# Eight experts on one core: four VectorE sums moved from the third to the fourth pair of column tiles, and a rare path moved from the middle to the end

## The chip, the cores and the metric

The kernel runs on one core of a Trainium2 chip, in one launch. The core has five engines that run their own instruction streams and meet at semaphores: TensorE (PE; its weight loads are shown as PEld), VectorE (DVE), ScalarE (ACT), GpSimd (POOL) and SyncE (SP, which here only issues DMA). The metric is the device time of one execution in microseconds (us). Before the change it is 427.3 us, the median of three runs (424.16, 427.3 and 427.44).

## The reference

Two stages follow each other. A gated recurrence, for 4 batches of 8 heads, gives 3072 tokens of 384 numbers; then every token is sent to one of 8 experts and through that expert's two layers:

```python
for t in range(S):                       # S = 768, head size 48
    state = alpha[:, :, t, :, None] * state + einsum('bhd,bhe->bhde', k[:, :, t], v[:, :, t])
    y[:, :, t] = einsum('bhd,bhde->bhe', q[:, :, t], state)
x = y as (3072, 384)
logits = normalized(x) @ normalized(expert_emb).T / tau      # 8 experts
expert_idx = argmax(logits); gate_w = softmax(logits)[expert_idx]
for e in range(8):
    mask = expert_idx == e
    h = maximum(x[mask] @ w1[e], 0.0)    # 384 -> 1024
    out[mask] = gate_w[mask, None] * (h @ w2[e])             # 1024 -> 384
```

All of it is float32.

## The kernel before, in words

**Stages.** Up to about 186 us the kernel computes the recurrence in 24 chunks of 128 tokens, chooses the experts, and writes each token's row to a place of its expert in a DRAM tensor `xs`. From there on `run(i)` works through the experts, i = 0 to 7, in an order of turns. The change lies in this second part; what follows is about it.

**One expert.** An expert has 384 rows (three tiles of 128), fetched from `xs` ahead of time. If it has more, `run_extra(i)` after it computes one further half block of 64 rows, behind a branch that every engine takes by a value read from memory (`values_load` of `extra`, L1156, and `tc.If`, L1160). With these data three of the eight experts take that half block: the first, the fourth and the fifth (i = 0, 3 and 4). The body that the other five jump over is 128 matmuls and 128 weight loads on TensorE. If an expert had more than one such half block, `run_rest` (L1164 to L1205) would compute the rest in a loop, behind one branch on `most` (L1169, L1173). With these data its body is never run. In the kernel before it stands after the fourth expert (i = 3); in program order there are four experts behind it.

**First layer, in pairs.** For i = 1 to 7, `first_layer_pair` (called at L1121) computes two of the eight 128-column tiles of the hidden layer, f and f + 4, with one of Strassen's schemes in place of the plain product: eleven products of 128x192, each two matmul records long in the trace, into four PSUM banks a, b, c, d. There are four such pairs, f = 0 to 3. The banks are drained by VectorE adds (`add`, at L919 in the trace, since the helper `by_dve` records them) and ScalarE copies and rectifiers (L1004, L1007). Each bank has a single buffer, so a later product into bank d waits for the add that reads d:

```python
product(c, s3, t3, True, False)
add(u3, c, u2)
filled(1)
product(d, c2, xT[:, 2, r2], True, False)
product(d, s1, t1, False, False)
add(h2[:, r2], d, u3)
filled(1)
...
product(d, s4, xT[:, 1, r2], False, False)
```

**The sums of the columns.** The second layer of two of the three tiles of rows is Strassen's scheme as well (`second_layer_pair`), and needs sums and differences of the hidden layer's columns, `hT_m`: four VectorE operations with two operands in SBUF for two values of f at a time (`mix_hidden`, 128x256 each). They wait in a list `fill`, and `filled(n)`, called inside `first_layer_pair`, takes n of them from the list: one, one and two in a pair. What is left at the end of the fourth pair is done there. `by_dve` ties every VectorE operation of this part to the one before it, so that they run in the order in which they are written.

**Beside it.** GpSimd computes sums of the second layer's weights for the same expert, `w2_m` (`mix_weights`, L943): eight operations on 128x384, from SBUF to SBUF, tied behind the last scatter of the expert before (`done_pair`). Between the pairs, TensorE turns a tile of the next expert's rows and VectorE copies it (`prepare`). After the fourth pair come the third tile of rows in plain form (`second_layer`, L903), the pair of tiles (L1044), and, on VectorE, the sums for the next expert's first layer (`mix_first`, L973).

Of the kernel before, what the change touches and what calls it, by code (L numbers as in the profile page):

```python
# [27 lines left out]
def kernel(  # L28
# [14 lines left out]
    E, DM = expert_emb.shape  # L43
# [8 lines left out]
    FT = F // P  # L52
# [76 lines left out]
    NW = 3  # L129
# [24 lines left out]
    def blocks_run(i):  # L154

        return NC - EARLY if i == 0 else NC

    def slots(i):
        return [(t, P) for t in range(blocks_run(i))] + [(blocks_run(i), HALF)]
# [40 lines left out]
    with ExitStack() as c1:  # L200
# [482 lines left out]
        for s in range(NS + 3):  # L683
# [57 lines left out]
            if 4 <= s < 4 + NXG * (NC + 1):  # L741
                i, t = divmod(s - 4, NC + 1)
# [39 lines left out]
    with ExitStack() as c3:  # L782
# [45 lines left out]
        def turn_of(calls):  # L828
            queue = ExitStack()
            for call in calls:  # L830
                queue.enter_context(tc.issue_after(call.ins))
            return queue
# [43 lines left out]
        def prepare(i, t, by=None):  # L876
            _, n = slots(i)[t]
            return turn(xg_s[i % NXG][:, t], xT_s[i % 2][:, :, t * P : t * P + n], n, by)

        def prepare_gates(i):  # L880
            n = len(slots(i))
            return gates(
                xg_s[i % NXG][:, 0:n], gt_s[i % NG][:, 0:n], sx_s[i % NG][:, 0:n], n,
                used[:, i, 0:n],
            )

        def first_layer(w1_t, hT, xT, f, n):

            ph = bank()[:, 0:n]
            for i in range(KT):  # L890
                nc.tensor.matmul(
                    ph, lhsT=w1_t[:, i, f * P : (f + 1) * P], rhs=xT[:, i],
                    start=(i == 0), stop=(i == KT - 1),
                )
            return nc.scalar.activation(hT[:, f], ph, AF.Relu)
# [19 lines left out]
        fill = []  # L915

        def by_dve(call, *args):
            with turn_of(dve):
                dve[:] = [call(*args)]  # L919
            return dve[0]  # L920

        def filled(n):
            for _ in range(min(n, len(fill))):
                fill.pop(0)()
# [8 lines left out]
        def mix_weights(w2_t, j):  # L933

            (b11, b12), (b21, b22) = quarters(w2_t)
            t1, t2, t3, t4 = (w2_m[:, k] for k in range(4))
            to, x, y = ((t1, b12, b11), (t2, b22, t1), (t4, b21, t2), (t3, b22, b12))[j]

            n = FT // 4
            with turn_of(done_pair):  # L940
                for k in range(2):
                    f = slice(k * n, k * n + n)
                    nc.gpsimd.tensor_tensor(to[:, f], x[:, f], y[:, f], ALU.subtract)  # L943

        def mix_hidden(hT, f0, f1):

            a11, a12, a21, a22 = (
                hT[:, j * FT // 2 + f0 : j * FT // 2 + f1, i * P : i * P + P]
                for i in range(2) for j in range(2)
            )  # L950
            s1, s2, s3, s4 = (hT_m[:, k, f0:f1] for k in range(4))
            for to, x, y, op in (
                (s1, a21, a22, ALU.add), (s2, s1, a11, ALU.subtract),
                (s4, a12, s2, ALU.subtract), (s3, a11, a21, ALU.subtract),
            ):
                yield lambda to=to, x=x, y=y, op=op: by_dve(nc.vector.tensor_tensor, to, x, y, op)
# [151 lines left out]
        def run(i):  # L1108

            w1_t, w2_t = w1_s[i % NW], w2_s[i % NW]  # L1110
            xT = xT_s[i % 2]
            n = blocks_run(i) * P
            nxt = slots(i + 1) if i + 1 < E else []
            hT = hp.tile([P, FT, NC * P], FP32, name="hT")[:, :, 0:n]
            pair = blocks_run(i) == NC
            dve[:] = [] if pair else ready
            if pair:
                for j in range(4):
                    mix_weights(w2_t, j)
                for f in range(FT // 2):  # L1120
                    done = first_layer_pair(w1_t, hT, xT, f)  # L1121
                    if f < len(nxt):
                        turned = prepare(i + 1, f, by_dve)
                    if f % 2 == 1:
                        fill.extend(mix_hidden(hT, f - 1, f + 1))
                filled(len(fill))
            else:
                for f in range(FT):
                    done = first_layer(w1_t, hT, xT[:, :, 0:n], f, n)
                    if f % 2 == 1 and f // 2 < len(nxt):  # L1130
                        turned = prepare(i + 1, f // 2)
            if nxt:
                with turn_of(dve):
                    mix_first(i + 1)
            if nxt:
                with tc.issue_after(done.ins), tc.issue_after(turned.ins):
                    prepare_gates(i + 1)
            else:

                with turn_of(done_pair):  # L1140
                    drained.append(nc.gpsimd.drain())
            gate, col = gt_s[i % NG], sx_s[i % NG]
            for t in range(2 if pair else 0, blocks_run(i)):
                sent = second_layer(
                    w2_t, hT[:, :, t * P : (t + 1) * P], gate[:, t : t + 1], col[:, t : t + 1]
                )
            if not pair:

                done_pair.append(sent)
            if pair:  # L1150
                second_layer_pair(w2_t, hT, gate, col)
# [14 lines left out]
        def run_rest(free):  # L1166

            w1_t, w2_t = w1_s[free], w2_s[free]
            big = nc.values_load(  # L1169
                most, min_val=0, max_val=N // HALF,  # L1170
                skip_runtime_bounds_check_because="the half blocks of an expert",
            )
            with tc.If(big > 1):  # L1173
                nc.sync.dma_start(out=turns[0:1], in_=extra)
                nc.sync.dma_start(out=turns[1:2], in_=turn_i)
                with tc.For_i(0, E) as i:

                    cur = yp.tile([1, 2], I32, name="cur", bufs=1)
                    for j in range(2):
                        nc.sync.dma_start(  # L1180
                            out=cur[0:1, j : j + 1], in_=turns[j : j + 1, ds(i, 1)]
                        )
                    e = nc.values_load(
                        cur[0:1, 1:2], engines=(SP,), min_val=0, max_val=E - 1,
                        skip_runtime_bounds_check_because="a sum of two experts, less E from E on",
                    )
                    nc.sync.dma_start(
                        out=w1_t, in_=w1_r[ds(e, 1)].rearrange("e p k f -> (e p) k f")
                    )
                    nc.sync.dma_start(  # L1190
                        out=w2_t, in_=w2_r[ds(e, 1)].rearrange("e p k d -> (e p) k d")
                    )
                    n = nc.values_load(
                        cur[0:1, 0:1], min_val=0, max_val=N // HALF - 2 * NC,
                        skip_runtime_bounds_check_because="the half blocks of an expert",
                    )
                    with tc.For_i(1, n) as u:
                        xg = yp.tile([P, 1, ROW], FP32, name="xg1", bufs=1)
                        nc.vector.memset(xg, 0.0)
                        nc.sync.dma_start(  # L1200
                            out=xg[0:HALF, 0], in_=xs[ds(e * N + u * HALF + NC * P, HALF)]
                        )
                        xT = yp.tile([P, KT, HALF], FP32, name="xT1", bufs=1)
                        turn(xg[:, 0], xT, HALF)
                        gate = yp.tile([P, 1], FP32, name="gate1", bufs=1)  # L1205
                        col = yp.tile([P, 1], I32, name="col1", bufs=1)
                        gates(xg, gate, col, 1)
                        half_block(w1_t, w2_t, xT, gate[0:HALF], col[0:HALF])
# [14 lines left out]
        for i in range(E):  # L1223
            if i + 2 < E:
                weights(i + 2)
                to_rows(pads[:, i + 2 : i + 3], blank)
                fetch(i + 2)
            run(i)
            run_extra(i)
            if i == 3:  # L1230
                run_rest(i % NW)


# [28 lines left out]
```

## Time and profile before

| what | measured |
|---|---|
| time, median of 3 | 427.3 us |
| span of the profiled execution | 428.2 us |
| TensorE matmul / weight load / VectorE / ScalarE / GpSimd busy | 97 / 85 / 64 / 42 / 45 % of the span |
| first expert product to the end | from about 180 to 428.2 us |

The times from the first product of a pair to the first product of the next one, in us (the last column to the first product of `second_layer`), read from the timeline of TensorE:

| expert | f = 0 | f = 1 | f = 2 | f = 3 | half block in f = 0 |
|---|---|---|---|---|---|
| i = 1 | 9.77 | 3.91 | 4.63 | 4.14 | yes (that of i = 0) |
| i = 2 | 4.29 | 3.90 | 3.91 | 4.00 | no |
| i = 3 | 4.29 | 3.91 | 4.24 | 4.00 | no |
| i = 4 | 10.89 | 3.90 | 5.55 | 4.01 | yes (that of i = 3) |
| i = 5 | 9.81 | 3.90 | 4.63 | 4.00 | yes (that of i = 4) |
| i = 6 | 4.29 | 3.91 | 3.90 | 4.00 | no |
| i = 7 | 7.89 | 3.58 | 3.57 | 3.58 | no |

The last expert has no rows of a next one to turn, so its pairs are some 0.33 us shorter. An expert's branch on `extra` lies behind the first products of the next expert, which is why the half block shows up in the next expert's f = 0.

How to read such a profile here: TensorE is busy nearly all of the time, so a change of the time has to show as a change of the gaps between its matmuls, or of the end behind the last of them. Work on the other engines counts only where a TensorE instruction waits for it.

### The profile page before, as it was taken

Reading aid. Unit: us, or ns where it says so; the run is one execution under the profiler, and the core shown is the slowest. Engines: PE = TensorE matmul, PEld = TensorE weight load, DVE = VectorE, ACT = ScalarE, POOL = GpSimd, SP = SyncE. Lnnn points to the kernel's source line nnn. Section 1 sums busy time; section 2 is a strip of 40 time slices with the busy share of each in tenths; the row PEclk is TensorE's granted clock in tenths of the full one; section 3 lists DMA queues with packets and bytes.
Section 4 is the critical chain, followed back from the end, with each engine's and each line's share of the span. In section 5 each row is a group of like instructions: output and inputs, shape, how many; then the busy total and the mean of one; then the engine's idle time right before and its main releaser. Section 6 shows DMA issues by size and latency. Waiting matters only on the chain. (4 is left out here: it accounts for less than half of the span.)

```text
span 428.2 us, 10643 instructions
## 1 busy us (share of the span) xinstructions
PE 414.1 (97%) x3962; PEld 365.2 (85%) x3962; DVE 274.4 (64%) x725; ACT 178.1 (42%) x430; POOL 191.6 (45%) x283
## 2 busy tenths in 40 slices
PE   8999999999999999999999999999899999997995
PEld 6988888898899876889799799798789979977984
DVE  7898788788798323816846837824862784782531
ACT  4455554554455335443523523613341362360410
POOL 7355776677765537208027036016302702604401
PEclk9999999999999999999999999999999999998999
DMA  9999999999979814869009129017304601001001
GB/s 141 157 159 160 149 209 162 213 182 211 194 167 342 315 63 132 269 222 337 2 35 344 38 60 349 8 50 273 96 20 155 237 2 55 2 14 40 0 17 38
DMA packets 119371, 60.15 MB, mean 140 GB/s; under 512 B 102287, under 2 KB 113816, under 8 KB 119312
## 3 DMA queue, kind: packets, MB, share of 16 engines
q1 hardware_dynamic: 115208, 49.14, 49.4%
q0 software_dynamic: 3728, 10.16, 6.7%
q8 instruction: 38, 0.62, 0.7%
q14 instruction: 21, 0.17, 0.1%
q10 hardware_dynamic: 376, 0.05, 0.1%
HBM read 49.69 MB, written 11.45 MB: 143 GB/s over the span
## 5 line engine op out<-in xcount | busy, mean ns | idle before, releaser
L814 POOL DMA_INDIRECT out_dram<-y,sx x25 | 24.4, 977 | 162.1 <-DVE xT_m L973 73.4
L996 PE MATMUL pq<-xT,w 128*128 128x192 f32 x280 | 65.6, 333 | 3.2 <-PEq L1160 2.6
L996 PEld LDWEIGHTS pq<-xT,w 128*128 128x128 f32 x280 | 48.2, 193 | 5.4 <-issue 3.5
L919 DVE TENSOR_TENSOR hT<-pq,v 128x192 f32<-128x192 f32 x84 | 29.8, 355 | 32.5 <-PE pq L996 30.1
L507 POOL TENSOR_TENSOR qs<-qc,a 128x512 f32<-128x512 f32 x24 | 30.6, 1276 | 35.9 <-DVE a L503 22.0
L903 PE MATMUL pyo<-w,hT 128*128 128x384 f32 x128 | 43.3, 492 | 0.0
L996 PE MATMUL pq<-xT_m,w_m 128*128 128x192 f32 x168 | 36.9, 329 | 0.3 <-PEq L1173 0.3
L903 PEld LDWEIGHTS pyo<-w,hT 128*128 128x128 f32 x128 | 23.7, 190 | 15.3
L1004 ACT ACTIVATE hT<-hT 128x384 f32<-128x384 f32 (+1 forms) x56 | 24.8, 443 | 26.9 <-DVE hT L919 22.3
L479 DVE TENSOR_TENSOR_SCAN r<-pa,inr 128x511 f32<-128x511 f32 x24 | 29.2, 1217 | 7.6 <-PE pa L194 5.9
L503 DVE TENSOR_TENSOR_SCAN a<-pa,ini 128x512 f32<-128x512 f32 x24 | 29.3, 1223 | 1.1
L996 PEld LDWEIGHTS pq<-xT_m,w_m 128*128 128x128 f32 x168 | 29.1, 192 | 0.6 <-issue 0.6
L1044 PE MATMUL pq<-w_m,hT_m 128*128 128x192 f32 x168 | 29.6, 326 | 0.0
L943 POOL TENSOR_TENSOR w_m<-w 128x384 f32<-128x384 f32 x28 | 27.7, 1011 | 3.6 <-DMA xs<-blank,pads 1.9
L1004 ACT ACTIVATE hT<-pq 128x192 f32<-128x192 f32 x28 | 9.2, 330 | 47.7 <-PE pq L996 47.7
L191 PE MATMUL sc<-qs,kr 64*128 64x128 f32 x384 | 28.7, 290 | 0.0
L313 POOL DMA_INDIRECT xs<-x,dest x24 | 24.4, 1016 | 8.2 <-issue 4.3
L1044 PEld LDWEIGHTS pq<-w_m,hT_m 128*128 128x128 f32 x168 | 27.7, 190 | 0.0
L191 PEld LDWEIGHTS sc<-qs,kr 64*128 64x128 f32 x384 | 24.1, 193 | 4.2 <-issue 3.0
L943 POOL TENSOR_TENSOR w_m<-w,w_m 128x384 f32<-128x384 f32 x28 | 27.1, 996 | 0.0
L191 PE MATMUL pyx<-sm,vt 128*64 128x128 f32 x384 | 26.3, 279 | 0.0
L1051 DVE SCALAR_TENSOR_TENSOR y<-pq,gt,u 128x192 f32<-128x192 f32 x21 | 8.8, 418 | 26.5 <-PE pq L1044 26.5
(199 smaller groups left out, 906.9 us busy)
## 6 DMA issues: line engine op xcount, KB each, us to landing
w<-in_moe_w_dram SPq DMA_DIRECT2D x16, 1536.0 KB
kt<-in_k_dram SPq DMA_DIRECT2D x24, 192.0 KB
qt<-in_q_dram SPq DMA_DIRECT2D x24, 192.0 KB
vt<-in_v_dram SPq DMA_DIRECT2D x24, 192.0 KB
xg<-xs SPq DMA_DIRECT2D x22, 196.5 KB
at<-in_alpha_dram SPq DMA_DIRECT2D x24, 168.0 KB
xg<-xs SPq DMA_DIRECT2D x8, 98.2 KB
at<-in_alpha_dram SPq DMA_DIRECT2D x24, 22.5 KB
```

The costliest lines, as they stand in the source:

```text
L191: last["pe"] = nc.tensor.matmul(*args, **kwargs)
L313: ins = nc.gpsimd.indirect_dma_start(out=xs, out_offset=bass.IndirectOffsetOnAxis(ap=rows, axis=0), in_=x, in_offset=None, bounds_check=E ...
L479: nc.vector.tensor_tensor_scan(r[:, L - 2 :: -1], pa[:, L - 1 : 0 : -1], inr[:, L - 2 :: -1], 1.0, ALU.mult, ALU.add,)
L503: d["a_scan"] = by_dve = nc.vector.tensor_tensor_scan(a, pa, ini, 0.0, ALU.mult, ALU.add)
L507: by_pool = nc.gpsimd.tensor_tensor(qs.rearrange("p n t -> p (n t)"), d["qc"], a, ALU.mult)
L814: ins = nc.gpsimd.indirect_dma_start(out=out, out_offset=bass.IndirectOffsetOnAxis(ap=col, axis=0), in_=y, in_offset=None, bounds_check=N - 1,
L903: pe[:] = [nc.tensor.matmul(py, lhsT=hT[:, f], rhs=w2_t[:, f], start=(f == 0), stop=(f == FT - 1),)]
L919: dve[:] = [call(*args)]
L943: nc.gpsimd.tensor_tensor(to[:, f], x[:, f], y[:, f], ALU.subtract)
L996: pe[:] = [nc.tensor.matmul(to, lhsT=left, rhs=right, start=start, stop=stop, skip_group_check=True,)]
L1004: return nc.scalar.activation(h, p, AF.Relu)
L1044: pe[:] = [nc.tensor.matmul(to, lhsT=left[:, f], rhs=right[:, f], start=start and f == 0, stop=stop and f == n - 1, skip_group_check=True,)]
```

## The change

The first edit moves the first group of four column sums: before, they were put into the list after f = 1, and so done during f = 2. Now they are put there after f = 2 and done during f = 3. The second group, of f = 2 and 3, is done after the fourth pair in both versions. The second edit moves `run_rest` behind the last expert, with that expert's weight buffer as the free one.

```diff
                     done = first_layer_pair(w1_t, hT, xT, f)
                     if f < len(nxt):
                         turned = prepare(i + 1, f, by_dve)
-                    if f % 2 == 1:
-                        fill.extend(mix_hidden(hT, f - 1, f + 1))
+
+                    if f >= FT // 4:
+                        f0 = 2 * (f - FT // 4)
+                        fill.extend(mix_hidden(hT, f0, f0 + 2))
                 filled(len(fill))
...
             run(i)
             run_extra(i)
-            if i == 3:
-                run_rest(i % NW)
+        run_rest((E - 1) % NW)
```

FT is 8, so `f >= FT // 4` holds for f = 2 (which puts in the sums of f = 0 and 1) and f = 3 (those of f = 2 and 3). The first edit is for another spread of VectorE's work over the pairs, the second for taking a path that is hardly ever used out of the middle of the program.

## The prediction

> **What bounds the kernel now.** I read the page's busy times first, then TensorE's waits from 180 us on (the experts), then what stands around each wait.
>
> ```profile
> PE 414.1 (97%) x3962; PEld 365.2 (85%) x3962; DVE 274.4 (64%) x725; ACT 178.1 (42%) x430; POOL 191.6 (45%) x283
> PE pq L996 <- PEq L1160: 2.6, 1, 2.6
> PE pq L996 <- DVE hT L919: 2.3, 3, 1.4
> PE pq L996 <- PEq L1173: 0.3, 1, 0.3
> ```
>
> TensorE is the bound. In the expert part it has three kinds of gap, and each concerns this change: a wait for VectorE's adds inside the pairs, one wait of 2.6 us at the branch on `extra` (L1160), one of 0.3 us at the branch of `run_rest` (L1173). Nothing else on TensorE can be won here.
>
> The gap inside the pairs is explained by what VectorE does just ahead of it. Expert i = 4, third pair (VectorE, then GpSimd, then TensorE):
>
> ```profile
> 300.41 2.49 DVE L919 TENSOR_TENSOR hT_m<-hT 128x256 f32<-128x256 f32 x1
> 302.82 0.34 DVE L919 TENSOR_TENSOR hT<-pq,v 128x192 f32<-128x192 f32 x1
> 300.67 1.94 POOL L943 TENSOR_TENSOR w_m<-w 128x384 f32<-128x384 f32 x2
> 303.22 0.92 PE L996 MATMUL pq<-xT,w_m 128*128 128x192 f32 x4 [1.38 <-DVE hT L919]
> ```
>
> The first moved sum takes 2.49 us; it ends when GpSimd's last `w2_m` operation ends (302.61). The add behind it, which frees bank d, comes late, and TensorE stands for 1.38 us. Over all experts the sums' median is 415 to 420 ns, but the first two of a group take up to 2487 and 950 ns, all in third pairs:
>
> ```profile
> L919 DVE TENSOR_TENSOR hT_m<-hT x28: 415/419/2487, 201.2 to 410.7; 128x256 f32<-128x256 f32 x28
> L919 DVE TENSOR_TENSOR hT_m<-hT_m,hT x14: 407/416/950, 203.0 to 409.9; 128x256 f32<-128x256 f32 x14
> ```
>
> The 2.6 us gap is one slow branch among eleven on TensorE's queue (minimum, median, maximum in ns), at 389.6 us; the next timeline row shows TensorE's restart, with matmuls at half their pace:
>
> ```profile
> L1160 PEldq COMPARE_BRANCH  x11: 70/193/3817, 182.6 to 421.2; - x11
> 393.61 0.98 PE L996 MATMUL pq<-xT,w 128*128 128x192 f32 x2 [2.63 <-PEq L1160]
> q8 instruction: 38, 0.62, 0.7%
> ```
>
> The other jumped branches on this line took 338 to 412 ns. The DMA line says why one could take ten times as long: 38 packets of 16 KB of instructions were fetched while the kernel ran, and one of them starts 1.0 us after this branch and ends 1.6 us before TensorE goes on.
>
> [...]adds with one operand in PSUM kept 0.36 us beside the same GpSimd work. [...]The eight matmuls from 393.6 to 396.3 us follow each other at 0.32 us and more, twice their usual 0.16.
>
> **Part 1, the sums.** Nothing is added or removed on any engine; four sums per expert (i = 1 to 7) go from f = 2 to f = 3. By the last `w2_m` operation's end, GpSimd is done before f = 3 starts in every expert: 202.49 against 204.18, 233.88 against 234.79, 263.91 against 265.59, 302.61 against 304.30, 339.32 against 341.01, 370.59 against 371.47, 400.90 against 404.88. So in f = 3 the sums take 0.42 us each. What they delay: in f = 3 VectorE has five adds of 0.36, one copy of 0.36 and now four sums of 0.42, together 3.84 us of the pair's 4.00. That is tight, but two of the sums stand behind the last add. And the trace has a case without contention: in i = 7, f = 2 has these sums at 0.41 us and is 3.57 us long, as its f = 3 without them (3.58). So TensorE loses nothing in f = 3. Behind f = 3 VectorE is about 0.83 us later (two sums). The first wait for it is the second product of the pair of tiles, 6.6 us after the end of f = 3 (for i = 5 from 345.01 to 351.57), while the last `hT_m` is done at 347.3, then at 348.2. `mix_first` ends at 352.0, then 352.8; the next adds start at 353.14 now, after 0.84 us of idle. The scatter behind L906 moves by as much; GpSimd has nothing else then. Cost: nothing. Gain: f = 2 falls to the 3.90 us of an undisturbed pair: 0.73 (i = 1) + 0.01 + 0.34 (i = 3) + 1.65 (i = 4) + 0.73 (i = 5) + 0 + 0 = 3.46 us.
>
> **Part 2a, the middle.** Expert i = 4's first pair takes 10.89 us; those of i = 1 and 5, with the same half block and no `run_rest`, 9.77 and 9.81. Taking the loads and branches out gives 1.1 us. The listing of the instructions also shows the last two `xs<-blank,pads` scatters move from behind that branch to the six at 163 to 170 us, where GpSimd then idles 2.49 us: 2 x 1.29 = 2.58, so the early tokens' scatter may start some 0.4 us later, and nobody waits for it. In f = 0 of i = 4, `w2_m` starts about 1 us earlier.
>
> **Part 2b, the slow branch.** [...]I counted instructions in the two compiled TensorE programs. The branch of `extra` jumps 259 instructions[...]. In the program before, the jumped branches of i = 1, 2, 5, 6, 7 stand at 5534, 6148, 8324, 8938 and 9512: modulo 256 at 158, 4, 132, 234 and 40. Only 234 was slow[...]. In the program after they stand at 159, 6, 59, 162 and 225.[...] The second reading, that a block had just begun and its successor wasn't there yet, or that labels don't count, puts i = 7 (225, or exactly the old place if labels fall away) in danger, but not i = 1, 2, 5 or 6; i = 7's branch has no matmul behind it. So the stall leaves the path. It is worth more than its gap: 7.89 us against the 3.96 that f = 0 of i = 6 (4.29) would have without its turn of 0.33; that is 3.93 us, the rest being the half clock.
>
> **Part 2c, the end.** After the change each engine reads `most` (269 to 311 ns in the middle) and jumps before the final waits. TensorE's jump there is 329 instructions from place 232: it likely [...]takes 3.8 us, from about 423.4 to 427.2 on the old time scale. Today the end is set by the last scatter's landing at 426.7 and ten SP waits to 427.3; TensorE would come through just then. GpSimd gains a load, a branch and a semaphore step (0.2 to 1.0 us) beside the same landing. I take +0.4 us; the bounds are 0 and +2 (both TensorE branches slow, or GpSimd's step in full with its 2.0 us drain behind).
>
> **Sum.** -3.46 - 1.1 - 3.93 + 0.4 = -8.1 us: 427.3 becomes 419.2.
>
> **Rivals.** (A) The slow fetch doesn't go but falls on another mid-program branch[...]: -3.46 - 1.1 + 0.4, 423.1 us.[...] Against it: four known places. (B) The third pair's gain is given back in the fourth, where VectorE's margin is 0.16 us: -1.1 - 3.93 + 0.4, 422.7. Against it stands i = 7. (C) The sums are not hidden in f = 3 at all: 7 x 4 x 0.42 = 11.8 us, and the end costs 2: -8.5 + 11.8 + 2 = +5.3, 432.6, slower. For it: 3.84 of 4.00 us; against it: the same load in f = 2 with a larger copy (i = 2) caused no gap, even with stretched sums.
>
> **How the numbers follow.** Forecast 0.75, (A) 0.10, (B) 0.07, (C) 0.05, unknown 0.03. The bounds of the end and of part 1 (a run of before came in at 424.2) give 416.8 to 421.5 for the forecast; with (A) and (B) the range is 416.8 to 423.4. Faster by over 1% means below 423.0: 0.82; same 0.12; slower 0.06.
>
> **What would show it.** All `hT_m` sums at 0.41 to 0.43 us; f = 2 at 3.9 us in each expert; f = 3 unchanged at 4.0; i = 4's f = 0 near 9.8; i = 7's near 4.0 with no branch over 0.5 us before 420 us; a slow branch on the `most` line at the end. It would be wrong with new TensorE waits for L919 in f = 3, a 3.8 us branch in mid-program, or a tail over 7 us behind the last matmul (5.3 now).

## The result and the profile after

The kernel after takes 420.02 us (median of four runs, 419.12 to 420.91) against 426.85 us for the kernel before on the same chip (four runs, 424.16 to 427.44). The ratio is 0.9852, with a 95% interval of 0.9804 to 0.9900: 6.8 us faster, where the forecast was 8.1.

The spans of the two profiled executions differ by more, 428.2 against 418.6 us: the trace of before is of an execution of 430.28 us, longer than all four timed ones, that of after of one of 420.33. They split as follows; each number is a difference of start or end times of TensorE's products in the two traces.

| stretch | before | after | difference |
|---|---|---|---|
| start to the first product of the pairs (i = 1) | 185.87 | 184.01 | -1.86 |
| from there to the end of the last product | 237.01 | 228.00 | -9.01 |
| from there to the end | 5.28 | 6.62 | +1.34 |

The change doesn't touch the first stretch; it varies between executions and chips, so what follows compares the second, called the **expert part**, and the third, the **tail**. The expert part by pairs (lengths from the first product of one pair to that of what follows, in us):

| pair | i = 1 | 2 | 3 | 4 | 5 | 6 | 7 |
|---|---|---|---|---|---|---|---|
| f = 0 before | 9.77 | 4.29 | 4.29 | 10.89 | 9.81 | 4.29 | 7.89 |
| f = 0 after | 9.65 | 4.28 | 4.29 | 9.66 | 9.66 | 4.29 | 3.96 |
| f = 2 before | 4.63 | 3.91 | 4.24 | 5.55 | 4.63 | 3.90 | 3.57 |
| f = 2 after | 3.91 | 3.91 | 3.90 | 3.91 | 3.90 | 3.91 | 3.57 |

f = 3 is 4.00 us in i = 1 to 6 of the kernel after and 3.58 in i = 7, as before (i = 1 had 4.14 then).

A part of this table isn't the change's. The half block in the first pairs of i = 1, 4 and 5 takes TensorE 5.74 to 5.91 us in the trace of before, but 5.62 each time in the kernel after and in every trace below but three; those three, from a second chip, have 5.70 to 5.96.

The busy times of the page of the kernel after and its line on instruction packets:

```profile
PE 408.0 (97%) x3962; PEld 361.1 (86%) x3962; DVE 267.9 (64%) x725; ACT 178.6 (43%) x430; POOL 191.3 (46%) x283
q8 instruction: 38, 0.62, 0.6%
```

The counts are what they were. VectorE's busy time has fallen by 6.5 us, though it does the same operations; TensorE's has fallen by 6.1, of which some 2.5 lie ahead of the pairs. The answer for the tile `hT_m` of the kernel after (minimum, median, maximum in ns) says where VectorE's fall comes from; these two groups have lost 6.45 us:

```profile
L919 DVE TENSOR_TENSOR hT_m<-hT x28: 411/416/419, 203.1 to 400.0; 128x256 f32<-128x256 f32 x28
L919 DVE TENSOR_TENSOR hT_m<-hT_m,hT x14: 411/414/424, 203.7 to 399.2; 128x256 f32<-128x256 f32 x14
```

The maxima of 2487 and 950 ns are gone: no sum in any expert is stretched. VectorE's timeline of i = 4, fourth pair, in the kernel after:

```profile
299.90 0.41 DVE L919 TENSOR_TENSOR hT_m<-hT 128x256 f32<-128x256 f32 x1
300.23 0.35 DVE L919 TENSOR_TENSOR hT<-pq,v 128x192 f32<-128x192 f32 x1
300.50 0.41 DVE L919 TENSOR_TENSOR hT_m<-hT_m,hT 128x256 f32<-128x256 f32 x1
```

The sum takes 0.41 us and the add that frees a bank follows at once. TensorE's waits from 180 us on have no row left in this trace: none for L919, none for a branch. TensorE's timeline at the start of i = 7 shows the place of the old 2.6 us gap:

```profile
383.23 0.81 PE L996 MATMUL pq<-xT_m,w_m 128*128 128x192 f32 x4
384.19 0.56 PE L996 MATMUL pq<-xT,w 128*128 128x192 f32 x2
```

0.15 us lie between the end of the first row and the start of the second, where 2.63 us were, and the products go on at their usual pace. The branches on TensorE's queue in the kernel after (L1162 is `extra`, L1175 is `most`, now at the end):

```profile
L1162 PEldq COMPARE_BRANCH  x11: 70/297/698, 180.8 to 410.3; - x11
L1175 PEldq COMPARE_BRANCH  x1: 1480/1480/1480, 412.6 to 412.6; - x1
```

The 3817 ns branch is gone from the middle. At the end there is one of 698 ns and one of 1480, not one of 3.8 us.

### The profile page after: what moved, and what is told of

Same layout as the page of the kernel before. It is cut to its first block, busy times and chain, and to the rows that moved or that the text cites. A ratio compares the mean times of both kernels' runs of the same rounds, so it can differ in the third digit from the quotient of the medians.

```text
span 418.6 us, 10657 instructions
## 1 busy us (share of the span) xinstructions
PE 408.0 (97%) x3962; PEld 361.1 (86%) x3962; DVE 267.9 (64%) x725; ACT 178.6 (43%) x430; POOL 191.3 (46%) x283
## 5 line engine op out<-in xcount | busy, mean ns | idle before, releaser
L996 PE MATMUL pq<-xT,w 128*128 128x192 f32 x280 | 64.5, 328 | 0.6
L919 DVE TENSOR_TENSOR hT<-pq,v 128x192 f32<-128x192 f32 x84 | 30.0, 357 | 32.8 <-PE pq L996 30.8
L996 PEld LDWEIGHTS pq<-xT,w 128*128 128x128 f32 x280 | 47.3, 190 | 2.8 <-DVEq L1162 1.7
L919 DVE TENSOR_TENSOR v<-pq,v 128x192 f32<-128x192 f32 x56 | 19.9, 356 | 9.1 <-ACT v L1007 4.4
```

What stands on the lines that cost most here:

```text
L996: pe[:] = [nc.tensor.matmul(to, lhsT=left, rhs=right, start=start, stop=stop, skip_group_check=True,)]
```

## The experiments

Each kernel is compared with the kernel before in runs on the same chip; the runs with two, four and sixteen idle products come from a second chip, the other experiments from a first. Five kernels do exactly the work of before or after, with only a few idle products put ahead of everything: they shift TensorE's code. "Place" is an instruction's number in the compiled TensorE program modulo 256, a count chosen by the author; in the traces of before and after 261 and 260 of TensorE's instructions start per 16 KB instruction packet (4171 from 16.17 to 145.12 us and 4159 from 16.30 to 143.96 us, over sixteen packets each, ahead of the first jump). From the sixteen idle products on it is counted without labels (the marks in the program to which branches jump), for a reason that appears there.

### Each half of the change by itself

The sums' edit alone, with the rare path left behind the fourth expert:

```diff
-                    if f % 2 == 1:
-                        fill.extend(mix_hidden(hT, f - 1, f + 1))
+                    if f >= FT // 4:
+                        f0 = 2 * (f - FT // 4)
+                        fill.extend(mix_hidden(hT, f0, f0 + 2))
```

> The sums are moved to the fourth pair, and run_rest stays behind i = 3. My theory: all hT_m sums take 0.41 to 0.43 us, f = 2 is 3.9 us in every expert, f = 3 stays at 4.0; that is 3.5 us. The first pair of i = 4 stays near 10.9. Each expert has one TensorE instruction more than before, so the branch of i = 6 stands at 240 of a block and not at 234. [...]f = 0 of i = 7 is 4.0 and the time is about 419.5 us. Rival (a block was entered just before, and its successor had not been fetched): the branch at 240 is still slow, over 2.5 us, and the time is about 423.4.

Measured: 419.9 us (before 426.88; ratio 0.9844, 0.9812 to 0.9877). Expert part 228.94 us, tail 5.26, f = 2 at 3.90 us in i = 1 to 6; the first pair of i = 4 takes 10.61 us, not 10.9. This kernel's answers on the tile `hT_m` and on the line of `extra`:

```profile
L919 DVE TENSOR_TENSOR hT_m<-hT x28: 412/415/419, 202.7 to 400.5; 128x256 f32<-128x256 f32 x28
```

The sums are as short as in the whole change.

```profile
L1162 PEldq COMPARE_BRANCH  x11: 70/197/415, 180.3 to 410.8; - x11
```

And the slow branch is gone too: the longest of the eleven, that of i = 6, now at place 240 instead of 234, took 415 ns.

The rare path's move alone:

```diff
-            if i == 3:
-                run_rest(i % NW)
+        run_rest((E - 1) % NW)
```

> run_rest at the end, the sums in the third pair as before. My theory: sums of up to 2.5 us in f = 2, f = 2 longer than 3.9 in some experts as before (3.4 us in all, less in i = 4, where w2_m starts earlier), no slow branch before the end (the jumped branches stand at 158, 4, 54, 156, 218), f = 0 of i = 4 at 9.7, and an end about 1.3 us longer than that of the kernel before: about 423 us. Rival (the gain of the change is all in the sums): about 427.

Measured: 423.53 us (ratio 0.9934, 0.9898 to 0.9969), expert part 231.06, tail 6.64. This kernel's answer on the tile `hT_m`:

```profile
L919 DVE TENSOR_TENSOR hT_m<-hT x28: 410/419/1577, 198.8 to 402.5; 128x256 f32<-128x256 f32 x28
```

Its branches on the lines of `extra` and `most`:

```profile
L1160 PEldq COMPARE_BRANCH  x11: 70/297/3321, 180.4 to 413.0; - x11
L1173 PEldq COMPARE_BRANCH  x1: 2799/2799/2799, 416.9 to 416.9; - x1
```

Its TensorE waits from 180 us on (in total, times, longest):

```profile
PE pq L996 <- DVE hT L919: 1.4, 3, 0.5
```

The stretched sums and the wait for L919 are there as in the kernel before, if less. The slow branch has left the middle here as well, and one of 3.3 us, which the forecast didn't have, stands at i = 7 (413.0 us), behind nearly all of TensorE's work. So each half removes the 3.93 us of i = 7's first pair by itself: the halves share that term and do not add. What is each half's own is 3.06 us for the sums (231.06 - 228.00) and 0.94 us for the path in the middle (228.94 - 228.00). The sums' term depends on the other edit: with the path moved, f = 2 of i = 4 is 4.62 us instead of 5.55, but that of i = 7 is 3.92 instead of 3.57. In the kernel before, i = 7 was spared only because TensorE's stall let GpSimd finish first (at 400.90 us, the sums starting at 402.96); without the stall a sum there takes 1192 ns.

### The kernel after without the rare path

```diff
-        run_rest((E - 1) % NW)
```

> The changed kernel without run_rest at all, which leaves out the rows that an expert has beyond its first half block over 384; with these data there are none. My theory: the loads, the branch and the semaphore steps at the end cost 0.3 to 0.4 us of the 1.3 us by which the end grew; the rest is the landing of the last scatter, which they do not cause: the distance from the last product to the end is 5.3 to 6.3 us, the time is 0.3 to 1.3 us under the changed kernel. Rival (they delay the scatter's landing): the distance is 5.3 as in the kernel before, and the landing comes 2.2 us after the scatter's start and not 3.4.

Measured: 419.0 us (ratio 0.9817, 0.9786 to 0.9848), expert part 228.01, tail 5.31. The forecast was wrong here: without the path the last scatter lands 2.23 us after its start, as in the kernel before. So the path does delay the landing, and the whole 1.3 us of the longer tail belong to it; by which of its parts is taken up below.

### Is it GpSimd's work or VectorE's own load?

The kernel before, but from i = 2 on GpSimd computes two of the four sums of the weights:

```diff
-                for j in range(4):
+                for j in range(4 if i == 1 else 2):
```

> The kernel before, but GpSimd computes only two of the four sums of the second layer's weights from the third expert on, so that those experts' second layer uses old sums: this leaves out part of the computation. GpSimd is then done before f = 2. My theory (the two engines contend): from i = 2 on all hT_m sums take 0.41 to 0.43 us though they are still in the third pair, and f = 2 is 3.9 us. Rival (VectorE has too much to do in the third pair, wherever GpSimd is): f = 2 stays at 4.2 to 5.6 us in i = 3, 4 and 5.

Measured, in a single run: 424.39 us. The sums stand in the third pair as before, and VectorE has all its work. GpSimd, though, is done before they start: in i = 4 at 295.90 us, the first sum starting at 297.52 (in the kernel before 302.61 and 300.41). The answer on the tile over the whole kernel:

```profile
L919 DVE TENSOR_TENSOR hT_m<-hT x28: 414/418/1590, 198.9 to 405.0; 128x256 f32<-128x256 f32 x28
```

The same from 210 us on, where GpSimd has half its work:

```profile
L919 DVE TENSOR_TENSOR hT_m<-hT x24: 414/417/426, 230.3 to 405.0; 128x256 f32<-128x256 f32 x24
```

In i = 1 a sum still takes 1590 ns and f = 2 takes 4.65 us; in i = 2 to 6 no sum exceeds 426 ns and f = 2 takes 3.90 to 3.91. The third pair was long because of what GpSimd did beside it. The slow branch stayed: 3344 ns at place 229.

### The slow branch: where the code lies

Two idle products ahead of the kernel **before** move all its branches by eight places, and change nothing else in the program:

```diff
+            for _ in range(2):
+                mm(pw[:, 0:8], lhsT=ident, rhs=ident[:, 0:8], start=True, stop=True)
```

> The kernel before with two more small matmuls at the very start, whose results nobody reads: they move every later TensorE instruction by 8 places. The branch of i = 6 then stands at 242 of a block and not at 234, those of i = 1, 2, 5, 7 at 166, 12, 140, 48. Theory ([...]from the runs so far blocks begin near place 206): at 242 the block was entered by the product before the last and the jump is fast: f = 0 of i = 7 is 4.0 and not 7.9, the sums and f = 2 stay as they were, about 423 us. Rival (the stall belongs to what i = 6 does, or to chance): 427.

Measured: 426.49 us against 429.43 (ratio 0.994, 0.9922 to 0.9959). The branches on the line of `extra` in this kernel:

```profile
L1162 PEldq COMPARE_BRANCH  x11: 70/197/415, 182.3 to 417.4; - x11
```

Its TensorE waits from 180 us on:

```profile
PE pq L998 <- DVE hT L921: 2.3, 3, 1.4
PE pq L998 <- PEq L1175: 0.3, 1, 0.3
```

The waits for the stretched sums are those of before, to the tenth; the 2.6 us at the branch are gone, and i = 7's first pair takes 3.96 us. Two idle products win what the change's largest single term won; the expert part is 233.52 us instead of 237.01 (f = 2 of i = 7 grows to 3.92 here too).

Sixteen of them in the kernel **after** were to bring the stall back, four to be harmless:

> The changed kernel with sixteen small matmuls at the start, whose results nobody reads: 64 places. The branch of i = 6 stands at 226, in the slow stretch, that of i = 1 at 223, those of i = 2, 5, 7 at 70, 123, 33. Theory of e5: the branch of i = 6 takes over 3 us again and f = 0 of i = 7 is near 7.9 us. If every instruction of the compiled stream holds a place, labels too, that of i = 1 is slow as well and f = 0 of i = 2 is near 8; if labels fall away, it is not. 424 to 428 us with one or two stalls. Rival (the change took the stall away by freeing the middle of the program): no slow branch, 420 to 421.5 us.

> Control for the one before: the changed kernel with four small matmuls at the start, 16 places. The branches of i = 1, 2, 5, 6, 7 stand at 175, 22, 75, 178 and 241, none in the slow stretch. All theories: no slow branch before the end; 419.5 to 421 us. The time of the small matmuls themselves, at most 0.2 us each, is the bound of what they add in the run with sixteen.

Measured: sixteen, 433.16 us (ratio 1.0129, 1.0056 to 1.0202); four, 427.84 (0.9959, 0.9941 to 0.9976), beside the same runs of before; both are longer than forecast. The line of `extra` with sixteen has one slow branch:

```profile
L1164 PEldq COMPARE_BRANCH  x11: 70/197/3960, 188.2 to 420.9; - x11
```

It is that of i = 6, as the count without labels has it (206); that of i = 1, at 223 with labels counted, took 0.46 us. So the count without labels is the one that fits. The first pair of i = 7 took 6.58 us and not 7.9: TensorE's gap was 2.76 us, as long as the old one, but the matmuls behind it follow each other at 0.16 us. The half clock that stands behind the gap of the kernel before (granted clock 0.50 from 393.4 to 396.5 us, matmuls 0.32 us apart) doesn't show in that pace. Four idle products left every branch in the middle at 0.42 us or less, and the expert part at 228.75 us. But both kernels start the experts late, with the first product of the pairs at 189.50 us (four) and 191.47 (sixteen) instead of 184.01, so that their whole times can't be set beside that of the kernel after. Four runs on the first chip, the kernel after once more, the sums' edit and two further shifts, look into this:

> The kernel after, unchanged, beside the others of this call. On the chip of the last call VectorE's first y of the routed rows (ahead of the experts) started 5 to 8 us after the add before it, in the kernel before with two idle products and in both kernels with more; on the first chip it started about 1.2 us after. If that is the chip, this run shows the late y or the early one together with the other three of this call; if it came from the idle products at the start, this run and the sums-only one show the early y (start of the experts near 184.0 us) and the two with idle products the late one (189 us or more). The expert part from the first product of the pairs to the last product: 228.0 us either way.

> The sums' edit alone (the rare path stays behind the fourth expert), beside the kernel after on one chip. If moving the rare path gains nothing net (about 1.0 to 1.2 us won in the middle, 1.3 us lost at the end), the two times agree within 0.3%; if the later landing of the last scatter was chance, the kernel after is 1.2 us faster (0.3%).

> The kernel after with ten idle products of eight columns ahead of everything: all branches 40 places later (labels not counted, i = 1 at 194, i = 2 at 38, i = 5 at 82, i = 6 at 182, i = 7 at 242). Theory: the jump is slow while the block after the one just entered is still on its way, so only from a place soon behind a block's start; slow so far 195, 197, 202, 206, quick 210 and more, and the start lies near 178. So i = 1 must now be slow (3.3 to 4.0 us instead of 0.36), with the first pair of i = 2 at 6.6 to 8.2 us instead of 4.29; i = 6 at 182 stands at the edge, either way. Expert part 228.0 plus 3 to 4 us (plus 6 to 8 if i = 6 is slow too). Rival: the slow branch belongs to i = 6 and what runs ahead of it there: then i = 1 stays at 0.36 us.

> The kernel after with eighteen idle products: two more than in the run with sixteen, all branches 8 places later than there (labels not counted, i = 6 at 214 instead of 206, i = 1 at 226, i = 7 at 18). Theory: 214 lies behind the slow stretch (202 to 206 slow, 210 quick in a kernel before), so no branch over 0.5 us in mid-program, the first pair of i = 7 at 3.96 us and not 6.58, expert part 228.0 us. Rival (the number of idle products or the code's length itself causes the stall): 3.9 us again at i = 6, expert part 232 us.

| kernel | us | ratio to before (426.6) | first pair starts, us | expert part, us | tail, us |
|---|---|---|---|---|---|
| after, again | 419.70 | 0.9846 (0.9809 to 0.9884) | 183.63 | 228.01 | 5.32 |
| sums' edit alone, again | 419.87 | 0.9852 (0.9815 to 0.9889) | 183.76 | 228.95 | 5.28 |
| after, ten idle products | 428.53 | 1.0048 (1.0024 to 1.0072) | 187.96 | 234.20 | 7.08 |
| after, eighteen | 427.11 | 1.0005 (0.9976 to 1.0035) | 187.73 | 228.01 | 6.44 |

The late start comes from the idle products: the first real product (L194 in the kernel after) starts at 4.70 us in the kernel after, at 5.8 with four, at 8.8 with ten and at 9.1 with eighteen. That is the idle products' own time: each is two matmul records, which start 0.21 us apart at first and 0.11 later on, so the 0.2 us of the forecast for each was too low. With four and with sixteen a second delay stands ahead of the experts, a 2.2 us wait of TensorE for VectorE's copy (L845), with VectorE idle for 8.2 and 8.4 us. On what VectorE waits isn't settled; it goes with the chip or the execution, not with the number of idle products, since VectorE idles for 5.2 to 5.4 us at that place with two and in the trace of before, and not with ten, with eighteen or in any other trace. The expert part is free of both, and there the theory's two forecasts hold: with ten, i = 1's branch (place 194) is slow; with eighteen, 214 instead of sixteen's 206, no branch in the middle is. The first pair of i = 2 with ten is 8.83 us, above the forecast of 6.6 to 8.2. Eighteen also settles the labels: counted with them, i = 6's branch would stand there at 234, the slow place of the kernel before. The line of `extra` with ten idle products:

```profile
L1164 PEldq COMPARE_BRANCH  x11: 70/192/4192, 184.7 to 420.5; - x11
```

The same line with eighteen:

```profile
L1164 PEldq COMPARE_BRANCH  x11: 70/192/444, 184.5 to 414.1; - x11
```

TensorE's timeline with ten, behind i = 1's branch and at the start of i = 7:

```profile
227.93 0.56 PE L998 MATMUL pq<-xT,w 128*128 128x192 f32 x2 [3.01 <-PEq L1164]
...
395.06 0.81 PE L998 MATMUL pq<-xT,w 128*128 128x192 f32 x4 [1.50 <-issue]
```

The first is the old gap at a new place, so the stall doesn't belong to i = 6. The second, 1.5 us, has no branch right in front of it: i = 6's branch (place 182) was quick, but TensorE stands a few products later. The packets tell both. In fifteen branches of 0.7 to 4.2 us in ten of these traces, TensorE's branch ends 1.32 to 1.50 us after the end of a 16 KB instruction packet, wherever the branch began. Some of these pairs, end of packet and end of branch, in us: in the kernel before 392.02 and 393.44, in the kernel after at its end 409.70 and 411.04, and 412.75 and 414.09, with ten idle products 226.26 and 227.76. The 1.5 us gap ends 1.46 us after a packet too (393.60 and 395.06). The same lag in all sixteen marks them as waits for code.

## Why the prediction was right, and where it wasn't

**Part 1, the sums: right in cause and size.** -3.46 us were forecast; f = 2 gave -3.44 and f = 3 of i = 1 another -0.14. The four sums cost f = 3 nothing, so rivals (B) and (C) are out. The halved GpSimd work shows the cause: the same sums, in the same place, with GpSimd's operations over before they start, are back at 0.42 us. The 84 adds with one operand in PSUM were never held in the trace of before (343 to 359 ns); by what the sums are held isn't shown. One sum took 2.49 us, longer than any single GpSimd operation there (about 1.0 us): it was held across several of them. It ends not with GpSimd's last operation, as the prediction has it, but 0.29 us behind (302.90 and 302.61), and so does the last stretched sum of i = 1, 2, 3, 5 and 6, by 0.28 to 0.29 us. And i = 7's f = 2, the prediction's case without contention, was free of it only through the stall that the change then removed; in f = 3 of the kernel after GpSimd is done in time in i = 7 as well (393.97 us, the first sum at 395.67).

**Part 2a, the middle: right.** -1.1 was forecast. i = 4's first pair fell by 1.23 us between the two traces, but against the sums' edit alone, on one chip, only from 10.61 to 9.66: the path's own is 0.94. The other 0.28, and the 0.27 by which the first pairs of i = 1 and 5 fell (9.77 to 9.65, 9.81 to 9.66), are the longer half blocks in the trace of before. The forecast took a little of that for the path, since i = 4's half block there (5.91 us) is 0.13 to 0.17 us longer than the two that it was compared with.

**Part 2b, the slow branch: right in size, wrong in reason.** 7.89 us became 3.96, the forecast 3.93 us less. But which places are slow was the author's estimate there, from 234 alone, and it is wrong: counted as there, the branches at 229 (halved GpSimd work) and 218 (the path's move alone) were slow as well. The prediction's second reading is what the runs support: a block, the code of one 16 KB packet, has just begun, and the block that the jump goes to isn't there yet. Without labels the slow places are 194 (ten idle products), 195 (the path's move alone), 197 (halved GpSimd work), 202 (before) and 206 (sixteen); 208 (the sums alone), 210 (before with two), 214 (eighteen) and 218 (i = 7 with four, i = 1 with sixteen) are quick (0.42 to 0.46 us). The slow places span thirteen; by the 260 or 261 instructions per packet, as an estimate, a jump of 259 from there ends in the very next block, and these jumps waited all the same. The wait is one packet of 0.9 to 1.6 us and 1.3 to 1.5 us behind it; in the five branches in the middle or at i = 7 that took 3.3 to 4.2 us, the packet started only 1.0 to 1.7 us after the branch. The warning that came with this reading, danger for i = 7 alone, was right as well: its branch, at 202, took 698 ns (801 in the second run, 825 without the path), ending 1.34 us after its packet. Why that packet started 2.0 us ahead of the branch, when the one of i = 6 before, at 202 too, came 1.0 us after the branch's start, isn't settled: the place alone doesn't decide.

Rival (A), the same stall at another branch, is a real danger: the runs with ten and sixteen idle products show it. The forecast was right by position, then, and not because the rare path moved: either half of the change, or two idle products, takes the stall away. That the 3.93 us came out is in part luck: the estimate on which they were argued was wrong, and only the reading kept beside it, which happened to give the same forecast, was right.

**Part 2c, the end: mis-sized.** +0.4 us were forecast, +1.34 measured, inside the bounds of 0 to 2. The forecast 3.8 us of TensorE's last branch were 1.48, since its packet had started 0.8 us ahead of it. GpSimd's added steps lie beside the landing, as forecast: in all seven traces with the path at the end they run from 0.8 to 1.7 us after the last scatter's start. That holds also for the one trace with a tail of 5.32 us, so it isn't they that lengthen it. The cost comes from a thing that the prediction didn't have. The bytes per slice of the kernel after from 413.0 to 417.5 us (40 slices of 0.11 us), and its instruction packet:

```profile
GB/s 573 369 287 232 260 0 27 0 0 0 0 0 0 0 0 41 678 328 287 287 164 0 0 0 0 41 0 0 0 41 0 27 0 0 0 0 0 0 0 0
q8 instruction: 1, 0.02, 1.5%
```

The same view, same stretch, of the second run of the kernel after:

```profile
GB/s 300 55 0 0 41 0 27 0 0 0 0 0 287 328 451 273 300 110 0 146 0 0 0 0 0 0 0 0 0 0 0 0 0 0 0 0 0 0 0 0
q8 instruction: 1, 0.02, 1.3%
```

In the first, the 16 KB packet starts within the last scatter (the 678, at 414.86 us) and ends at 415.92. Most of the scatter has landed by 415.5; three packets of it, the single 41, 41 and 27 behind, begin only at 415.91 and finish at 416.64. In the second run the packet comes later (the lone 146, at 415.16), behind the scatter's last byte at 415.10, and nothing trails. From the scatter's start to its landing it is 3.40 us in the first and 2.23 in the second; the tails are 6.62 and 5.32. Over all traces: in the seven with the path at the end, the landing took 3.23 to 3.96 us in six, and 2.23 in the one whose packet came behind it; in the six without, 2.22 to 2.24. In each of the six late ones the first trailing packet begins within 0.02 us of the code packet's end, and the landing comes 0.73 to 0.85 us behind that end, whether the code packet starts 1.18 or 2.12 us into the scatter. That three packets of the scatter queue behind the code on one of the DMA engines is what these times suggest; the trace used here doesn't name the engine, and no run moved the code packet alone.

This also says where the rare path's 0.94 us went: given back in the tail in six of the seven traces. The sums' edit alone is as fast as the whole change (419.90 against 420.02 and 419.87 against 419.70); the kernel after without the path, 419.0, is 0.9 us under the sums' edit of the same runs, but it leaves the path out.

**The difference from 8.1 to 6.8 us.** The profiled pair has -9.01 + 1.34 = -7.7 us in what the change touches. 0.55 us of it are the longer half blocks in the trace of before (0.27 + 0.28), which leaves -7.1. The rest lies in the spread of the runs, whose interval (0.9804 to 0.9900 of 426.85 us) is -8.4 to -4.3 us.

## What to carry to other kernels

VectorE sums of two SBUF operands took up to 2.49 us beside GpSimd's work here and 0.42 us one pair later; such a move by one stage is worth a try, if that stage has room: no operation was taken away, and 3.1 to 3.6 us came free. A gap at a branch (2.63 us), or a few products behind one (1.50 us), belonged to the code's position here: before a gain is put down to an edit, shift the code by two idle products and look again; one term of 3.9 us here went to whichever edit shifted it. And the branch moved to the end, where nobody seemed to wait, still fetched code: that packet fell among the last output's in six of seven traces, and the landing took 3.23 to 3.96 us there against 2.23.

## What the runs showed that I had not expected

- Where a 16 KB instruction packet of 1.0 to 1.3 us fell among the last scatter's packets, the landing came 1.0 to 1.7 us later (3.23 to 3.96 against 2.23).
- TensorE's wait for code ends 1.32 to 1.50 us after the packet does, and needs no branch right in front of it (the 1.5 us gap of the run with ten idle products).
- Idle products of eight columns at the very start are not free: with ten, the first real product starts 4.1 us later, with two 0.5 us.
- Half the clock didn't follow every such gap: behind 2.63 us (before, granted clock 0.50) the matmuls started 0.32 us apart, behind 2.76 us (sixteen idle products) 0.16.
